# A fused attention and feed-forward kernel: two groups of transposes moved from TensorE to DMA, the loads of the next batch moved forward, half chunks widened to 128 rows

## The chip, the cores and the metric

The kernel runs on one core of one Trainium2 chip. The metric is the device time of one execution in microseconds (us). A time is the median of several executions; a profile is one execution, and its span is about 2 us shorter than the device time. "Before" is the tuned kernel, "the changed kernel" has the change.

## The reference

```python
# attention: batch 8, heads 8, sequence 576, head dimension 64
theta = pi/2 * pos / S
phi(x) = concat(relu(x) * cos(theta), relu(x) * sin(theta))     # 128 features
kv  = einsum('bhsf,bhsd->bhfd', phi(k), v);  z = sum_s phi(k)
num = einsum('bhsf,bhfd->bhsd', phi(q), kv); den = einsum('bhsf,bhf->bhs', phi(q), z)
x   = (num / den) as (4608 tokens, 512)
# feed-forward
out = ((x @ w1) * (x @ w2)) @ w3 @ w_out        # 512 -> 1024 -> 1024 -> 512
```

The inputs are float32, the kernel computes in bfloat16 and gives float32.

## The kernel before

A batch is worked in five chunks of its sequence: four of 128 rows and one of 64, the half chunk, whose number is 4. The features of q and x have to be transposed, so that the features and not the rows of the sequence lie across the partitions. TensorE (PE) does it as a matmul against the identity, followed by a copy out of PSUM, or a DMA does it. The feed-forward part (FFN) works in nine tiles of 512 tokens; the attention of later batches is threaded between its matmuls at fixed slots.

```python
def order_of(b):
    return [0, 1, 2, 3, 4] if b % 2 == 0 else [4, 0, 1, 2, 3]

def dma_q(b):                        # chunks of q that a DMA transposes
    return order_of(b)[5 if b == 0 else 2 if b == 1 else 0:]

def num(b, c):                       # shortened
    nt = ps_att.tile([P, 2, 512], FP32, name="pnum")      # one buffer
    for h in range(H):
        nc.tensor.matmul(nt[...], lhsT=qpT[:, h, ds(at, 128)], rhs=kvs[:, h, :], ...)
    # VectorE: den = nt[.., 64] + 1e-6; reciprocal; xblk[rows] = nt[rows] * den

def x_tr(b, c):                      # shortened
    if b >= 2:
        nc.sync.dma_start_transpose(out=xT[t][:, :, ds(o, R)], in_=xf)
        return
    for kc in range(4):
        nc.tensor.transpose(pst[:, kc, 0:R], xf[:, ts(kc, 128)], identb[rows, rows])
    copy(out=xT[t][:, :, ds(o, R)], in_=pst[:, 0:4, 0:R])
...
# the last tile: its stores go out by SyncE and ScalarE in turn
if t == NT - 1:
    store((nc.sync, nc.scalar)[ms % 2], osb[:, ms % 2:ms % 2 + 1, :], 4 * t + ms, 1)
```

## Time and profile before

| | before |
|---|---|
| device time, median | 249.42 us in 3 runs; 249.39 with a fourth, beside the changed kernel |
| span of the profile | 247.4 us |
| PE busy | 239.9 us, 97% |
| VectorE / ScalarE / GpSimd busy | 57% / 50% / 38% |
| PE in the chain that ended last | 92% |
| matmuls of 512 columns | start 216 ns apart |
| transposes of 128 columns | start 56 ns apart |

The chain follows back from the last instruction to whatever released each step. Where it consists of PE pieces that touch, PE is the bound. (Ends of matmuls are modelled and overlap, so in a timeline I reckon with 216 ns per matmul of 512 columns and not with the length shown.) In the notation of the profile "PE ffnps L464 x8" is eight matmuls of line 464 that write the tile ffnps, SPq is an issue by SyncE, and the bracket at the end of a line of a timeline is how long the engine stood idle before it and what ended that.

### The profile page before, as it was taken

How to read it: one execution, taken by the hardware profiler on the slowest of the kernel's cores; microseconds unless marked ns; L12 is line 12 of the kernel's file. 1: busy time of each engine (PE TensorE's matmuls, PEld its weight loads, DVE VectorE, ACT ScalarE, POOL GpSimd, SP SyncE). 2: the span in 40 equal slices, each digit the busy share in tenths (PEclk: the TensorE clock that was granted, in tenths of full speed). 3: DMA queues.
4: the chain of work that ended last, by engine and by line, in shares of the span. 5: the costliest groups of instructions: out<-in, count | busy, mean ns of one | idle time of the engine just before them, and what ended most of it. 6: DMA issues, size and time to landing. Idle time of an engine off the chain costs nothing.

```text
span 247.4 us, 4896 instructions
## 1 busy us (share of the span) xinstructions
PE 239.9 (97%) x1808; PEld 127.5 (52%) x1839; DVE 141.9 (57%) x333; ACT 123.2 (50%) x209; POOL 94.3 (38%) x189
## 2 busy tenths in 40 slices
PE   8899999999999999999999999999999999999994
PEld 2478555565554445544544455455545554444443
DVE  7776674656657555748465966566586555312421
ACT  2676325927852594267426832783287332323331
POOL 7755241215512442154113621562143008878100
PEclk9999999999999999999999999999999999999999
DMA  6999999999999999999989899999985938999413
GB/s 195 179 193 199 210 204 205 144 160 190 181 119 194 138 154 133 149 158 174 124 134 151 112 153 153 153 181 146 141 108 150 185 82 170 305 300 303 154 41 130
DMA packets 86087, 41.15 MB, mean 166 GB/s; under 512 B 53552, under 2 KB 82608, under 8 KB 86064
## 3 DMA queue, kind: packets, MB, share of 16 engines
q0 software_dynamic: 37072, 27.20, 72.7%
q1 hardware_dynamic: 48560, 13.18, 33.4%
q10 hardware_dynamic: 432, 0.46, 0.5%
q8 instruction: 14, 0.23, 0.4%
q14 instruction: 9, 0.07, 0.1%
HBM read 38.80 MB, written 9.44 MB: 195 GB/s over the span
## 4 chain that ended last, share of the span: by engine, by line
PE 92%; DMA 3%; issue 1%; DVE 1%; POOL 1%; ACT 0%; POOLq 0%
PE ffnps L464 50%; PE ffnps L510 24%; PE ffnps L232 5%; PE pnum L355 4%; PE pnum L297 4%; DMA qs<-in_q_dram 3%; PE pst L220 2%; PE pst L392 1%; PE pst L328 1%; PE ffnps L527 1%; POOL vs L112 0%; DVE xblk L365 0%; PE pfirst L355 0%; ACT xT L394 0%; DVE xT L394 0%
## 5 line engine op out<-in xcount | busy, mean ns | idle before, releaser
L505 DVE TENSOR_TENSOR abT<-asb,ffnps 128x512 bf16<-128x512 bf16 x68 | 46.6, 685 | 56.1 <-PE ffnps L464 55.9
L464 PE MATMUL ffnps<-xT,w1b 128*128 128x512 bf16 (+2 forms) x310 | 74.4, 357 | 0.9 <-ACT xT L394 0.2
L464 PE MATMUL ffnps<-xT,w2b 128*128 128x512 bf16 (+2 forms) x312 | 74.0, 357 | 0.4
L510 PE MATMUL ffnps<-w34b,abT 128*128 128x512 bf16 x271 | 64.7, 379 | 0.4
L501 ACT CAST asb<-ffnps 128x512 bf16<-128x512 f32 x68 | 39.8, 585 | 49.8 <-PE ffnps L464 48.4
L516 ACT COPY held<-ffnps 128x512 f32<-128x512 f32 x35 | 20.5, 586 | 49.6 <-PE ffnps L510 43.6
L464 PEld LDWEIGHTS <-w1b 128*128 128x128 bf16 x320 | 28.9, 98 | 27.7 <-issue 0.6
L464 PEld LDWEIGHTS <-w2b 128*128 128x128 bf16 x320 | 28.7, 98 | 26.9
L510 PEld LDWEIGHTS <-abT 128*128 128x128 bf16 x280 | 25.6, 98 | 26.4
L269 ACT ACTIVATE qp<-qs,sinv 128x512 bf16<-128x512 bf16 (+2 forms) x40 | 28.3, 715 | 2.1 <-DMA qs<-in_q_dram 2.0
L365 DVE TENSOR_TENSOR xblk<-pnum,den 128x512 bf16<-128x512 f32 (+1 forms) x39 | 26.9, 691 | 2.2
L269 ACT ACTIVATE kp<-ks,sinv 128x512 bf16<-128x512 bf16 (+1 forms) x35 | 24.5, 720 | 0.0
L438 POOL DMA_DIRECT2D out_dram<-held x42 | 22.1, 532 | 4.6 <-DMA out_dram<-held 1.8
L540 POOL COPY seen<-xblk 64x1 bf16<-64x1 bf16 x15 | 2.7, 183 | 53.4 <-DVE xblk L365 53.4
L355 PEld LDWEIGHTS <-qpT 128*128 128x128 bf16 x320 | 15.0, 98 | 10.2 <-issue 2.7
L540 POOL COPY seen<-qp 64x1 bf16<-64x1 bf16 x14 | 2.6, 183 | 40.6 <-DVE qp L265 40.6
L265 DVE TENSOR_SCALAR qp<-qs,cosv 128x512 bf16<-128x512 bf16 (+1 forms) x40 | 17.2, 434 | 1.2 <-DMA qs<-in_q_dram 1.2
L363 DVE TENSOR_SCALAR den<-pnum 128x8 f32<-128x8 f32 (+1 forms) x39 | 6.4, 164 | 19.4 <-PE pnum L355 19.4
L289 POOL COPY va<-vs 128x512 bf16<-128x512 bf16 (+1 forms) x30 | 17.5, 632 | 0.0
L297 PEld LDWEIGHTS <-kp 128*128 128x128 bf16 x280 | 13.0, 98 | 7.3
L355 PE MATMUL pnum<-kvs,qpT 128*128 128x65 bf16 x312 | 16.4, 194 | 0.2
L232 PE MATMUL ffnps<-woutb,w3T 128*128 128x512 bf16 x61 | 15.0, 379 | 0.1
(87 smaller groups left out, 184.2 us busy)
## 6 DMA issues: line engine op xcount, KB each, us to landing
out_dram<-held POOLq DMA_DIRECT2D x16, 256.0 KB, 4.6
out_dram<-held POOLq DMA_DIRECT2D x24, 128.0 KB, 3.9
qs<-in_q_dram POOLq DMA_DIRECT2D x10, 256.0 KB, 5.6
w3b<-in_moe_w_dram POOLq DMA_DIRECT2D x8, 256.0 KB, 13.4
ks<-in_k_dram POOLq DMA_DIRECT2D x8, 256.0 KB, 6.0
vs<-in_v_dram POOLq DMA_DIRECT2D x8, 256.0 KB, 6.4
ks<-in_k_dram POOLq DMA_DIRECT2D x6, 320.0 KB, 5.5
qs<-in_q_dram POOLq DMA_DIRECT2D x6, 320.0 KB, 5.3
```

What stands on the lines that cost most here:

```text
L232: nc.tensor.matmul(acc[:, :], lhsT=w3T[:, lc, :], rhs=woutb[:, lc, :], start=(lc == 0), stop=(lc == 7))
L269: nc.scalar.activation(out=dst[:R, c, 0:n, D:F], in_=src[:R, 0:n, c, :], func=ACTF.Relu, scale=sinv[:R, at:at + 1], bias=0.0)
L289: eng.tensor_copy(out=feat_of(b)[2][:R, c, :, 0:D], in_=raw[b, "v"][:R, :, c, :])
L297: nc.tensor.matmul(kvt[:, h // 4, ds((h % 4) * 65, 65)], lhsT=kp[:, c, h, :], rhs=va[:, c, h, 0:D + 1], start=(i == 0 and h % 4 == 0), sto ...
L355: nc.tensor.matmul(nt[:, h // 4, ds((h % 4) * 65, 65)], lhsT=qpT[:, h, ds(at, 128)], rhs=kvs[:, h, :], start=True, stop=True)
L365: nc.vector.tensor_tensor(out=xblk[rows], in0=n4[:, :, :, 0:D], in1=den[rows].unsqueeze(3).to_broadcast([R, 2, 4, D]), op=ALU.mult)
L438: eng.dma_start(out=rows[:, :, cols], in_=osb[64 * i:64 * i + rows.shape[0], :, cols])
L464: nc.tensor.matmul(out, lhsT=w[:, kc, ts(jc, 128)], rhs=x[:, kc, tok], start=(kc == 0), stop=(kc == 3))
L501: nc.scalar.copy(out=asb[:], in_=aT[:, :])
L505: nc.vector.tensor_mul(out=abT[:, jc, :], in0=asb[:], in1=bT[:, :])
L510: nc.tensor.matmul(ops[:, :], lhsT=abT[:, jc, ts(ms, 128)], rhs=w34b[:, jc, :], start=(jc == 0), stop=(jc == 7))
L516: nc.scalar.copy(out=osb[:, ms % 2, :], in_=ops[:, :])
```

## The change

The intent is to shorten PE's stream: batch 1 takes its half chunk second instead of first, so that four of its five query chunks can go by DMA (a); x of its chunk 3 goes by DMA too (b); the x transposes of the two half chunks on PE use 128 rows instead of 64 (c); keys, values and queries of batch 2 are loaded sooner (d).

```diff
@@ other_loads
         load(1, "qv")
+        load(2, "k", 0)
@@ order_of, dma_q
+        if b == 1:
+            return [0, 4, 1, 2, 3]
-        return order_of(b)[5 if b == 0 else 2 if b == 1 else 0:]
+        return order_of(b)[5 if b == 0 else 1 if b == 1 else 0:]
@@ num
+        if b < 2 and c == 4:
+            rows, R = slice(0, P), P
+            n4 = nt[rows, :, 0:260].rearrange("p g (h e) -> p g h e", e=65)
@@ x_tr
+        xa = xblk[:].rearrange("p g h d -> p (g h d)")
-        if b >= 2:
+        if b >= 2 or b == 1 and c == 3:
-            nc.tensor.transpose(pst[:, kc, 0:R], xf[:, ts(kc, 128)], identb[rows, rows])
+            nc.tensor.transpose(pst[:, kc, :], xa[:, ts(kc, 128)], identb[:])
-        copy(out=xT[t][:, :, ds(o, R)], in_=pst[:, 0:4, 0:R])
+        copy(out=xT[t][:, :, ds(o, R)], in_=pst[:, 0:4, rows])
@@ slots of batch 1
-                         nu=(15, 17, 19, 20, 25), xt=(20, 20, 21, 22, 27))
+                         nu=(15, 17, 19, 20, 25), xt=(20, 20, 21, 22, 25))
-            for i in range(2):
-                between[11 + i].append(lambda i=i: behind_q(1, 2 + 2 * i, 2, "k", i))
-            for i, g in enumerate((15, 17, 17, 19)):
-                between[g].append(lambda i=i: behind_x(1, (i + 1) // 2, 2, "vvqq"[i], i % 2))
+            between[10].append(lambda: behind_q(1, 0, 2, "k", 1))
+            between[14].append(lambda: behind(att[1]["kvs"][0:64, 0, 0:1], 2, "v", 0))
+            for i, g in enumerate((15, 17, 17)):
+                between[g].append(lambda i=i: behind_x(1, (i + 1) // 2, 2, "vqq"[i], (1, 0, 1)[i]))
```

## The prediction

> **What bounds the kernel now.** I read the page's busy shares first, then the chain that ended last, then the chain and the timelines around 28 to 31 us and 44 to 82 us, where the change acts.
>
> ```profile
> PE 239.9 (97%) x1808; PEld 127.5 (52%) x1839; DVE 141.9 (57%) x333; ACT 123.2 (50%) x209; POOL 94.3 (38%) x189
> PE 92%; DMA 3%; issue 1%; DVE 1%; POOL 1%; ACT 0%; POOLq 0%
> ```
>
> The first line is busy time by engine, the second the shares of the chain. TensorE (PE) is both the busiest engine and 92% of the chain; VectorE, ScalarE and GpSimd are each under 60%. Busy time alone would not prove it, since matmuls overlap in the pipeline, so I looked at the rhythm in the chain (start, length, what):
>
> ```profile
> 46.71 0.45 PE pst L220 x8
> 48.02 0.45 PE pst L328 x8
> 48.47 0.86 PE ffnps L232 x4
> 49.33 0.45 PE pst L328 x8
> 49.78 0.86 PE ffnps L232 x4
> 50.64 1.27 PE pnum L297 x40
> ```
>
> Each piece starts where the one before ends: four matmuls of 512 columns take 0.86 us (216 ns each), eight transposes of 128 columns 0.45 us (56 ns each). There is no wait here. So PE streams columns without a pause, and a column removed from its stream is time off the end, provided that no operand comes late. The trace's start times say the same over the whole run: apart from lost records, from 31 us to the end I find pauses over 60 ns at only a dozen places, together about 1.5 us. The kernel has no 2% (5.0 us) to give in the part that the change touches.
>
> **What the Trainium skill says.** "TensorE: Matmul & The Clock Gate", section "Step-by-step: what each phase is for", gives 215.7 ns between matmuls of 512 columns and 55.6 ns for 128; the trace agrees (216 and 56). (The section after it says 131 and 81 for real kernels; this trace does not show that.) Its section "Part 4: PE-mode transpose" gives some 275 ns for a 128x128 transpose in a kernel. That is the duration of one; the trace has 219 ns for it, and in a stream they start 56 ns apart, so 56 ns is what I charge. "TensorEngine Tiling (Array Packing)", "Key Properties", says that changing the tiling mode drains TensorE. The trace agrees: the 64-row transposes of a half chunk are surrounded by two gaps (below). "DMA: Bandwidth & Descriptors", "Issuing engines are not separate DMA queues", says that all queues end on the same 16 DMA engines and interleave; the trace agrees, as a DMA transpose of q issued among loads landed after 6.3 us (median), among fewer after 3.0.
>
> **The change part by part.** I set the order of each engine's instructions against that of before. On PE 12 of 1839 matmuls (and their weight loads) go and 8 get wider. On the DMA queue of SP two transposes come in. VectorE loses one copy, ScalarE one copy, GpSimd one tiny copy.
>
> *(a) The half chunk of q of batch 1 by DMA.* Eight transposes of 128 columns go at about 49.3 us: 8 x 56 ns = 0.45 us, all of it PE stream, as the lines above show. VectorE loses a 0.42 us copy. The copy of the 128-row chunk (0.68 us) now stands ahead of the v copies, which ended at 50.24; by VectorE's line they would start about 49.25 (when the second half of v lands, 49.24) and the first be done at 49.6, the last about 50.45. PE reaches the kv matmuls about 50.1 and eats one chunk in 0.26 us, so it wants the last at 51.1. No wait.
>
> *(b) x of chunk 3 of batch 1 by DMA.* Four transposes go:
>
> ```profile
> 64.54 1.03 PE L464 MATMUL ffnps<-xT,w2b 128*128 128x512 bf16 x4
> 64.73 0.69 DVE L365 TENSOR_TENSOR xblk<-pnum,den 128x512 bf16<-128x512 f32 x1
> 65.47 0.23 PEld L392 LDWEIGHTS <-xblk 128*128 128x128 bf16 x4 [0.40 <-DVE xblk L365]
> 65.47 0.40 PE L392 MATMUL pst<-identb,xblk 128*128 128x128 bf16 x4
> ```
>
> In this timeline the matmuls from 64.54 are streamed by 64.54 + 4 x 0.216 = 65.40, but the transposes start at 65.47, just after xblk is written (65.42): a wait of 0.07 us. With it go 4 x 56 = 0.22 us. Saved: 0.29 us. This x belongs to the third 512-token tile of the FFN, read far later (about 109 us), so the DMA has 40 us.
>
> *(c) Half chunks with 128 rows.* Two places, batch 0 at 30.24 us and batch 1 at 57.88:
>
> ```profile
> 29.28 1.03 PE L464 MATMUL ffnps<-xT,w1b 128*128 128x512 bf16 x4
> 30.24 0.29 PE L392 MATMUL pst<-identb,xblk 64*128 64x64 bf16 x4
> 30.46 1.04 PE L464 MATMUL ffnps<-xT,w2b 128*128 128x512 bf16 x4
> ```
>
> The stream before ends at 29.28 + 0.86 = 30.14; the next begins at 30.46. The half chunk costs 0.32 us, though its 4 x 64 columns are only 0.12: two gaps of about 95 ns as the array changes its rows. With 128 rows the columns double to 4 x 56 = 0.22 and the gaps go: 0.09 us saved. In batch 1 the same 0.09 is saved in the stream but not in time: the next matmuls of PE write the one pnum buffer, and wait for VectorE to have normalized the chunk before. That xblk write ends at 58.26 and they start at 58.40, after a pause of 0.06 already; the pause just grows. So (c) is worth 0.09, not 0.18. VectorE's operations on 128 partitions instead of 64 cost the same (0.69 and 0.68 us).
>
> *(d) Loads of batch 2 sooner.* These move no PE work and PE waits for no load after 20 us in this trace, so alone they are worth nothing. They matter as room for (a), and because PE will want everything 0.8 us sooner:
>
> ```profile
> 38.23 0.68 POOL L137 DMA_DIRECT2D vs<-in_v_dram  x1 [0.97 <-DMA ks<-in_k_dram]
> 47.07 0.18 POOL L540 COPY seen<-qp 64x1 bf16<-64x1 bf16 x1 [8.16 <-DVE qp L265]
> 47.52 0.68 POOL L133 DMA_DIRECT2D ks<-in_k_dram  x1 [0.27 <-issue]
> ```
>
> GpSimd issues nothing for eight microseconds, waiting for a q feature, and the DMA engines run dry: between 48.0 and 49.5 us they moved 33 GB/s, against 176 just before. The lower half of k now follows v directly and fills that hole, the upper half follows at about 47.5 instead of 48.9, and v and q come about 2 us sooner, one step of the attention each.
>
> Sum: 0.45 + 0.29 + 0.09 = 0.83 us, 249.42 - 0.83 = 248.59.
>
> **The rivals.** *First: the DMA transposes of q come late.* There are now four in a row, the half chunk first, with deadlines of about 54.2 (half), 56.2 (chunk 1) and 57.9 (chunk 2), which are the starts of before less 0.45. Before, chunks 1, 2 and 3 were issued at 48.2, 49.6 and 52.3 and landed at 54.5, 57.6 and 58.5, so chunk 2 landed only 0.8 us before its use at 58.40. ScalarE now has its feature of chunk 1 about 0.6 us later, since the half chunk's 0.72 us activation no longer runs before the upper half of q lands, and SP issues the half chunk before it. Against it: the three landings were slow because both halves of k came in between (52.2 and 57.0); k will be through by about 52. But v of batch 2 now comes in from 53 to 58. If chunk 2 is late, it costs 0.3 to 1.2 us and most of the gain is gone: 248.9 to 249.6. I give it one in four. *Second: the pauses of batch 2 change.* PE stood 0.16, 0.07 and 0.16 us at 76.0, 78.1 and 80.2, each time until VectorE had normalized the chunk before; the order there is unchanged, and the same pauses recur in later batches, so I expect them to stay. Should a shift by 0.8 us remove them, 248.2. *Third: the gain is taken back downstream,* by a load or store that does not move with PE: against it, later loads are all triggered by the compute, and the chain has no DMA in it after 12 us. It would give 249.3 or so. *Fourth: VectorE or ScalarE bounds this stretch,* for (c) it does; for (a) and (b) the PE lines show no such wait.
>
> **Range and chances.** From 248.59 I move up 0.06 for the first rival: 248.65. The low end is the full gain, both halves of (c) and some of the pauses gone; the high end is a late transpose that takes nearly all. The runs of before lie within 0.4 us, which adds to both ends: 248.1 to 249.4. A gain or loss of 2% needs 5 us, and nothing here is of that size, so within 2% is nearly certain.
>
> **What would show it.** Twelve fewer matmuls and weight loads on PE; kv matmuls of batch 1 starting about 0.5 us sooner, near 50.1 in the chain; no 64-row transposes; a pause before the fourth num group of batch 1 grown from 0.06 to about 0.15; everything from 70 us on about 0.8 us sooner; the hole in DMA at 48 us filled. I am wrong if PE pauses at the num groups of the half chunk or of chunks 1 and 2 of batch 1 on the landing of a q transpose, if the v copies hold the kv matmuls, or if PE's later pauses grow by what was saved.

## The result, and the profile after

The changed kernel took 249.0 us (248.8 to 249.21, four runs), the kernel before 249.39 us (249.21 to 249.6, four runs). The ratio is 0.9984, with a 95% interval from 0.9967 to 1.0001. A ratio is the mean time of one kernel's runs over that of the other's of the same rounds, so it is not quite the ratio of the medians. Some 0.4 us were gained where 0.8 was expected. In two later groups of runs the unaltered changed kernel came out at 1.0004 and 0.9998 of the kernel before, so even the 0.4 us are not certain.

First, what the page of the changed kernel says (busy time, then the shares of the chain):

```profile
PE 241.2 (98%) x1827; PEld 127.2 (51%) x1827; DVE 142.1 (57%) x332; ACT 122.5 (50%) x208; POOL 93.9 (38%) x188
PE 92%; DMA 3%; DVE 1%; issue 1%; POOL 1%; ACT 0%; POOLq 0%
```

PE looks busier although it does less: the trace of before has 1808 of 1839 matmuls, here all 1827 are recorded. A comparison of busy sums would mislead by more than the effect, so I compare start times. The chain of the changed kernel, around the transposes that went (start, length, what):

```profile
46.92 0.45 PE pst L221 x8
47.37 0.86 PE ffnps L233 x4
48.23 0.45 PE pst L331 x8
48.68 1.73 PE ffnps L233 x8
50.40 1.27 PE pnum L300 x40
```

One group of eight transposes is left where there were two, and eight matmuls now run in one piece. From the start of those transposes to the kv group it is 2.17 us (48.23 to 50.40); before it was 2.62 us (48.02 to 50.64). That is 0.45 us for (a), and the v copies cause no wait. The timeline around the half chunk of batch 0, and the one around the last x of batch 1:

```profile
29.59 1.03 PE L472 MATMUL ffnps<-xT,w1b 128*128 128x512 bf16 x4
30.46 0.39 PE L400 MATMUL pst<-identb,xblk 128*128 128x128 bf16 x4
30.68 1.03 PE L472 MATMUL ffnps<-xT,w2b 128*128 128x512 bf16 x4
```

```profile
64.30 1.03 PE L472 MATMUL ffnps<-xT,w2b 128*128 128x512 bf16 x4
64.48 0.69 DVE L372 TENSOR_TENSOR xblk<-pnum,den 128x512 bf16<-128x512 f32 x1
65.16 0.81 PE L472 MATMUL ffnps<-xT,w1b 128*128 128x512 bf16 x3
65.20 1.19 SPq L395 DMA_TRANSPOSE xT<-xblk  x1
```

In the first, four transposes take 0.22 us and both neighbours touch them: 29.59 + 0.86 = 30.45. The two gaps are gone. In the second, PE goes straight from one group of matmuls to the next (64.30 + 0.86 = 65.16) while SyncE issues the transpose. And GpSimd's loads:

```profile
38.48 0.68 POOL L137 DMA_DIRECT2D vs<-in_v_dram  x1 [0.57 <-DMA ks<-in_k_dram]
39.85 0.68 POOL L133 DMA_DIRECT2D ks<-in_k_dram  x1 [0.69 <-DMA ks<-in_k_dram]
46.85 0.18 POOL L548 COPY seen<-qp 64x1 bf16<-64x1 bf16 x1 [6.32 <-DVE qp L268]
47.30 0.68 POOL L137 DMA_DIRECT2D ks<-in_k_dram  x1 [0.27 <-issue]
```

The lower half of k follows v at 39.85 instead of 47.52, and between 48.0 and 49.5 us the DMA engines moved 170 GB/s instead of 33.

So every expected step is there. To see where the gain ended, I cut the span at five places that can be found in every trace: the first FFN matmul, the first kv group of batch 2, the last matmul, the landing of the last store, the end (us; the table also has the experiments told below).

```
                     first FFN   to kv of   to last   to last   to the    span
                     matmul at   batch 2    matmul    landing   end
before                 15.85      51.59     176.63     2.34      0.99    247.40
changed                16.16      50.74     176.62     2.32      1.36    247.19
after_again            15.92      50.74     177.27     2.33      1.34    247.59
after_third            15.51      50.74     179.32     2.33      1.35    249.24
after_tiny7            15.91      50.73     177.45     2.36      0.92    247.37
after_pool_store       15.82      50.73     176.84     2.35      0.93    246.67
after_pool_store2      15.82      50.74     176.99     2.38      0.93    246.86
after_late_x           15.76      50.73     176.79     2.36      0.92    246.55
after_no_b27           16.08      51.04     176.63     2.31      0.92    246.98
after_no_b             15.74      52.77     176.62     2.32      0.93    248.37
after_no_d             16.03      54.68     177.60     2.32      1.35    251.97
before_tiny2           15.92      51.59     176.63     2.38      1.34    247.86
part_c                 15.79      51.49     177.27     2.34      0.98    247.86
part_b                 15.61      51.28     176.99     2.33      0.92    247.13
```

Second column: the change took 51.59 - 50.74 = 0.85 us off PE's stream, against 0.83 predicted, and it did so in every execution, within 0.01 us. Last column but one: 0.37 us of it are lost after the last store has landed. The start of this one execution was 0.31 us later. The third column is the same here, but not in the repeats.

The 0.37 us after the landing can be followed in the semaphore instructions of SyncE at the end. In these traces the hardware DMAs (those issued by SyncE and ScalarE) take eight completion semaphores in turn. At the end SyncE waits for all of them in a fixed order, one after another, about 62 ns each where nothing is outstanding. Times at which these waits ended:

```
semaphore     1st     2nd     3rd     4th     5th     6th     7th     8th    last landing
before      244.67  244.73  244.79  245.74  246.11  246.28  246.45  246.52   246.41 (7th)
changed     245.88  245.94  246.00  246.07  246.13  246.19  246.25  246.31   245.83 (1st)
```

The change adds two hardware DMAs, so the last store moves two places on, from the seventh semaphore past the eighth to the first. Before, SyncE had done six of the eight waits when the last store landed; now all eight are still to do. The summary of SyncE's waits shows the same in one line each, before and changed (us in total, times, longest):

```profile
SPq L690 <- DMA out_dram<-held: 1.2, 2, 0.9
```

```profile
SPq L698 <- DMA out_dram<-held: 1.8, 1, 1.8
```

Before, the two waits counted are those on the fourth and the fifth semaphore (0.90 and 0.32 us in the trace); those for the last two stores, 0.13 us each, are too short for this view. In the changed kernel it waits once, 1.8 us, on the first of the eight, and by then all others are done.

### The profile page after: what moved, and what is told of

Same layout as the page of the kernel before. It is cut to its first block, busy times and chain, and to the rows that moved or that the text cites. A ratio compares the mean times of both kernels' runs of the same rounds, so it can differ in the third digit from the quotient of the medians.

```text
span 247.2 us, 4909 instructions
## 1 busy us (share of the span) xinstructions
PE 241.2 (98%) x1827; PEld 127.2 (51%) x1827; DVE 142.1 (57%) x332; ACT 122.5 (50%) x208; POOL 93.9 (38%) x188
## 4 chain that ended last, share of the span: by engine, by line
PE 92%; DMA 3%; DVE 1%; issue 1%; POOL 1%; ACT 0%; POOLq 0%
PE ffnps L472 50%; PE ffnps L518 24%; PE ffnps L233 6%; PE pnum L358 4%; PE pnum L300 4%; DMA qs<-in_q_dram 3%; PE pst L221 1%; PE pst L400 1%; PE ffnps L535 1%; PE pst L331 1%; POOL vs L112 0%; DVE xblk L372 0%; PE pfirst L358 0%; ACT xT L402 0%; DVE xT L402 0%
## 5 line engine op out<-in xcount | busy, mean ns | idle before, releaser
L472 PE MATMUL ffnps<-xT,w2b 128*128 128x512 bf16 (+2 forms) x320 | 74.9, 357 | 0.0
L518 PE MATMUL ffnps<-w34b,abT 128*128 128x512 bf16 x280 | 65.8, 379 | 0.0
```

Of the source, the lines that this page charges most:

```text
L472: nc.tensor.matmul(out, lhsT=w[:, kc, ts(jc, 128)], rhs=x[:, kc, tok], start=(kc == 0), stop=(kc == 3))
L518: nc.tensor.matmul(ops[:, :], lhsT=abT[:, jc, ts(ms, 128)], rhs=w34b[:, jc, :], start=(jc == 0), stop=(jc == 7))
```

## The experiments

My theory after the result (the closing theory): PE's stream gained 0.85 us as predicted, and 0.37 to 0.43 us went to the order of the closing waits. The rivals: the start got slower by 0.31 us through the change; or the difference is noise; or, as the prediction feared, late DMA transposes take the gain back in the middle.

### First group: the closing waits

**after_again** is the changed kernel once more.

> The changed kernel, unaltered, as the yardstick of this group. Both theories: ratio to before 0.998 (0.997 to 1.000). Closing theory: from the landing of the last store to the end of the span 1.36 us again, with eight more semaphore waits of SyncE after that landing. Start theory (the changed kernel lost 0.3 us because its first load of k landed at 7.32 instead of 6.76 us): if the change did that, it lands near 7.3 again and PE's first FFN matmul starts near 16.15; if it is scatter from run to run, it moves.

Measured: 249.34 us (249.07 to 250.7, 6 runs), before 249.37 (248.86 to 251.31, 11 runs), ratio 1.0004 (0.9977 to 1.0030). Landing to end 1.34 us. The first load of k landed at 6.85 us and PE's first FFN matmul was at 15.92. In a third profile of the same kernel, told below, they were 6.45 and 15.51. The start is scatter: the rival of the start falls. But this execution lost 0.65 us in the third column. By the start times PE stood 0.25 us before the third FFN tile (at 85.4 us) and 0.38 us before the fourth (at 109.0), each time until a DMA transpose of x had landed; more on this in the third group.

**after_tiny7** adds seven useless DMAs, to turn the semaphores on by seven.

```diff
     load_first4(nc.sync, k0, k)
+    junk = const.tile([16, 7, 16], FP32, name="junk")
+    for i in range(7):
+        nc.sync.dma_start(out=junk[:, i, :], in_=q[0, 0, ds(16 * i, 16), 0:16])
```

> The changed kernel with seven DMAs of 1 KB each, whose data nobody reads, issued by SyncE behind the first loads, so that the last store of the output takes the eighth of the eight completion semaphores of the hardware queues instead of the first. Closing theory: SyncE has one wait left after the last landing instead of eight, landing to end 0.93 us instead of 1.36, and the time about 0.4 us under the changed kernel's, 248.6, ratio to before 0.9966. Rival (the missing gain went to the start or to noise): the time of the changed kernel, 249.0, ratio 0.998 to 0.999.

Measured: 249.26 us (248.47 to 249.7), ratio 0.9988 (0.9963 to 1.0012). Landing to end 0.92 us, with one wait left, as the theory has it. The time of 248.6 did not come: in the profiled execution 0.83 us were lost in the third column. The closing part of the expectation held, the time did not show it.

**after_pool_store** reaches the same without extra DMAs.

```diff
-                store((nc.sync, nc.scalar)[ms % 2], osb[...], 4 * t + ms, 1)
+                store((nc.gpsimd, nc.scalar, nc.sync)[ms], osb[...], 4 * t + ms, 1)
```

> The changed kernel with the first store of the last 512-token tile issued by GpSimd instead of SyncE. There is one hardware DMA fewer, so the last store again takes the eighth semaphore, without any extra DMA. Closing theory: landing to end 0.93 us, time about 248.6, ratio 0.9966, and the same as with the seven small DMAs. Rival: 249.0, or slower if GpSimd's store lands last.

Measured: 248.83 us (248.59 to 249.72), ratio 0.9981 (0.9956 to 1.0007). Landing to end 0.93 us; GpSimd's store landed at 242.0 us, well before the others. The median is 0.51 us under that of after_again, in the right place, but the intervals overlap.

**before_tiny2** gives the kernel before the two extra hardware DMAs and nothing else (the same edit as in after_tiny7 with 2 in place of 7).

> The kernel before with two DMAs of 1 KB, whose data nobody reads, issued by SyncE behind the first loads: as many more hardware DMAs as the change adds, and nothing else of it. Closing theory: the last store takes the first semaphore, landing to end goes from 0.99 to 1.36 us, time 249.75, ratio 1.0015, while PE's stream is as before. Rival: no change, ratio 1.0000.

Measured: 249.68 us (249.3 to 250.45), ratio 1.0011 (0.9988 to 1.0034). Landing to end 1.34 us instead of 0.99, the stream 51.59 us as before. So two DMAs that move 2 KB lengthen the closing by 0.35 us in the profile. In all fourteen traces the closing follows from the last store's semaphore alone: 0.92 to 0.93 us on the eighth, 0.98 to 0.99 on the seventh, 1.34 to 1.36 on the first. That part is shown, for profiled executions; the device times agree in direction but are too wide to show it by themselves.

### Second group: the parts

**part_c**, the kernel before with the widened half chunks alone (the edits of num and of the PE branch of x_tr above).

> The kernel before with (c) alone: the two half chunks of x with 128 rows. By the prediction's reckoning 0.09 us off PE's stream at 30 us (first FFN matmul to first w3 transpose 16.26 instead of 16.35 us) and nothing at 58 us, where the pause before the fourth num group of batch 1 grows from 0.06 to about 0.16 us. No DMA is added, so landing to end stays 0.99 us. Ratio to before 0.9996, too little for the times to show. Rival (both half chunks pay): 0.18 us in the stream.

Measured: 249.42 us against 249.23 for before on this chip, ratio 1.0004 (0.9985 to 1.0022). The stream is 0.10 us shorter, all of it at 30 us; at 58.2 us the pause is 0.17 us. So one half chunk pays and the other does not, and the rival falls. The profiled execution also had a pause of 0.46 us at 177.6 us on a late DMA transpose of q: such pauses come without the change's DMAs too.

**part_b**, the kernel before with x of chunk 3 of batch 1 by DMA.

```diff
-        if b >= 2:
+        if b >= 2 or b == 1 and c == 3:
```

> The kernel before with (b) alone: x of chunk 3 of batch 1 by DMA. Stream 0.29 to 0.30 us shorter between the last num group of batch 1 and the first kv group of batch 2. One hardware DMA more, so by the closing theory the last store takes the eighth semaphore and landing to end is 0.93 us instead of 0.99. Sum 0.36 us, ratio 0.9986: nearly all of what the whole change gained in the record's times. Rival for a cost of (b): the transpose stands ahead of those of q of batch 2 on SyncE, so chunk 1 of that q, which landed 2.3 us before its use in the kernel before, has 1 us or less left, and in some executions PE waits for it.

Measured: 249.27 us, ratio 1.0002 (0.9977 to 1.0026). The stream is 51.59 - 51.28 = 0.31 us shorter and the closing 0.92 us, both as expected. But the time does not show the 0.36 us. The profile has the cost that the rival named: chunk 1 of q of batch 2 landed at 75.03 instead of 73.74 us, 0.46 us before its use, and at 80.03 PE waited 0.34 us more than usual for another chunk:

```profile
PE pnum L355 <- DMA qpT<-qp: 0.3, 1, 0.3
```

**after_no_b**, the changed kernel with the line of part_b undone.

> The changed kernel without (b): x of chunk 3 of batch 1 on PE again. PE's stream is 0.30 us longer than the changed kernel's, and one hardware DMA goes, so by the closing theory landing to end falls from 1.36 to 0.93 us: the time comes out about 0.13 us under the changed kernel's though PE does more work; stream 0.55 us shorter than before, ratio to before 0.9975. Rival (closing order does not matter): 0.3 us slower than the changed kernel. The landing of chunk 1 of q of batch 2 should again be 1.5 us or more ahead of its use.

Measured: 250.14 us (249.92 to 250.85), ratio 1.0039 (1.0012 to 1.0065). Slower than the kernel before, and than the changed kernel in each of its groups, against the expectation. The list of PE's waits names the cause:

```profile
PE pst L400 <- DVE xblk L372: 1.6, 1, 1.6
```

The experiment was wrong. The change had also moved this x from slot 27 to slot 25, right behind its own num group. A DMA doesn't mind, but PE then stands and waits until VectorE has normalized the chunk. Closing: 0.93 us, as expected. A part has to be undone together with the place that was chosen for it.

**after_no_d**, the changed kernel with the loads of batch 2 where the kernel before has them (the first part of the diff and the loads in its last part undone).

> The changed kernel without (d): k, v and q of batch 2 loaded when the kernel before loaded them. If (d) is the room that (a) needs: chunk 2 of q of batch 1 lands after 58 us and PE pauses 0.3 to 1 us at its num group, the DMA engines move about 33 GB/s between 48.0 and 49.5 us as before, ratio to before 0.999 to 1.002. If (d) is worth nothing: stream as in the changed kernel, landing to end 1.36 us, ratio 0.998.

Measured: 251.59 us (250.53 to 253.86), ratio 1.0102 (1.0043 to 1.0162). The first theory holds, and the cost is larger than I expected: by the medians, of different groups, (d) is worth some 2.5 us to the changed kernel. The profiled execution is the longest of the four (253.86 us); its stream to batch 2 is 3.94 us longer than the changed kernel's. The busy time by stretch (PE, its weight loads, VectorE, ScalarE, GpSimd, then the granted clock, the DMA share and GB/s), and one line of PE's timeline:

```profile
56.20:58.70 2.50, 0.26 (x2) 0.00 (x0) 0.00 (x0) 0.80 (x2) 1.65 (x4) 1.00 1.57 102
58.70:60.60 1.90, 1.84 (x20) 1.37 (x21) 1.30 (x4) 0.65 (x2) 0.11 (x1) 0.84 1.38 212
60.60:63.60 3.00, 2.78 (x20) 1.74 (x19) 1.35 (x5) 1.91 (x5) 1.62 (x4) 0.53 1.57 134
```

```profile
58.76 0.43 PE L357 MATMUL pnum<-kvs,qpT 128*128 128x65 bf16 x8 [2.30 <-DMA qpT<-qp]
```

It was chunk 1, not chunk 2, that came late: its transpose, issued at 49.37 us, landed at 58.72 us, while both halves of k came in. PE stood 2.3 us, and then its granted clock fell: 0.53 on average from 60.60 to 63.60 us, where matmuls of 512 columns started up to 427 ns apart. The expectation didn't contain that. From 48.0 to 49.5 us the DMA engines moved 32 GB/s: the hole is back.

```profile
48.00:49.50 1.50, 1.50 (x15) 0.91 (x14) 1.27 (x3) 1.50 (x3) 1.30 (x3) 1.00 0.20 32
```

### Third group: what (b) costs, and two versions that beat the kernel before

**after_third** is the changed kernel again.

> The changed kernel, unaltered, as the yardstick of this group. Landing to end 1.36 us, eight waits of SyncE after the last landing; stream from the first FFN matmul to the first kv group of batch 2 50.73 us (51.59 before). Ratio to before 0.998 to 1.000.

Measured: 249.09 us (248.57 to 251.3), before 249.14 (249.05 to 250.98, 11 runs), ratio 0.9998 (0.9963 to 1.0034). The stream to batch 2 and the closing are as expected. The profiled execution was the longest one, of 251.3 us, and shows why (PE's waits, and its timeline):

```profile
PE ffnps L472 <- DMA xT<-xblk: 2.3, 2, 1.6
```

```profile
82.62 2.32 PE L518 MATMUL ffnps<-w34b,abT 128*128 128x512 bf16 x10
86.56 1.02 PE L472 MATMUL ffnps<-xT,w1b 128*128 128x512 bf16 x4 [1.61 <-DMA xT<-xblk]
```

The third FFN tile could not start, because two x transposes of batch 2 landed at 86.2 and 86.4 us, 8.8 and 7.5 us after their issue. In the first profile of the same kernel PE started that tile at 85.38, and the last of these transposes had landed at 85.18:

```profile
82.78 2.75 PE L518 MATMUL ffnps<-w34b,abT 128*128 128x512 bf16 x12
85.38 1.03 PE L472 MATMUL ffnps<-xT,w1b 128*128 128x512 bf16 x4
```

**after_no_b27** undoes (b) with its slot.

```diff
-        if b >= 2 or b == 1 and c == 3:
+        if b >= 2:
-                         nu=(15, 17, 19, 20, 25), xt=(20, 20, 21, 22, 25))
+                         nu=(15, 17, 19, 20, 25), xt=(20, 20, 21, 22, 27))
```

> The changed kernel without (b), this time with the place of the transposes restored too: the change had also moved x of chunk 3 next to its own num group, which is harmless for a DMA but makes PE wait 1.8 us for VectorE (that spoiled the first trial). Now the transposes stand two steps later, as in the kernel before. Closing theory: stream 0.55 us shorter than before, landing to end 0.93 us, ratio 0.9975 to 0.9985, at least as fast as the changed kernel although PE does 0.3 us more. Rival: 0.3 us slower than the changed kernel.

Measured: 248.60 us (248.56 to 248.93, 6 runs), ratio 0.9968 (0.9945 to 0.9990). The stream is 51.59 - 51.04 = 0.55 us shorter than before and the closing 0.92 us. PE does 0.30 us more than in the changed kernel, and the kernel is faster than before by an interval that leaves out 1, which none of the three groups of the changed kernel did. The gain is 0.3%, far under 2%. Its six runs lie within 0.4 us, those of the changed kernel beside it within 2.7; but those of before, also without (b), lie within 1.9, so the spread alone does not point at (b). No wait on a DMA stands in its list of PE's waits.

**after_pool_store2** is after_pool_store once more.

> The changed kernel with the first store of the last tile issued by GpSimd, once more, beside the changed kernel on one chip. Closing theory: landing to end 0.93 us, 0.43 us under the changed kernel, ratio to before 0.9966 to 0.998. Rival: no better than the changed kernel.

Measured: 248.98 us (248.32 to 249.35), ratio 0.9976 (0.9948 to 1.0004). Closing 0.93 us. The median is only 0.11 us under after_third's; the mean is 0.57 us lower, but much of that is the one run of 251.3 us. This version has the same closing as after_no_b27, and so is the fairer one to hold it against: without (b) the median is 0.38 us lower and the mean 0.20, though PE does 0.30 us more. The runs of the two overlap, so this is a hint and not a proof that (b) costs more than it saves.

**after_late_x** is after_pool_store with x of chunk 3 issued behind the q transposes of batch 2.

```diff
+            if b == 2 and i == 0:
+                plan[z + 7].append(lambda: x_tr(1, 3))        # and no longer at slot 25
             plan[z + 7 + 2 * i].append(lambda c=c: x_tr(b, c))
```

> The same, and the DMA transpose of x of chunk 3 of batch 1 issued behind those of q of batch 2 instead of ahead of them. If its place in the queue is what made chunk 1 of q of batch 2 late (landing 0.2 to 0.3 us before its use, once 0.2 us after it): that chunk lands about 1.3 us before its use, and PE does not wait for it. Risk: the three x transposes of batch 2 that the third FFN tile reads at 85.4 us go out later, and PE may wait there 0.1 to 0.5 us. Landing to end 0.93 us. Ratio 0.996 to 0.998 if the risk stays out.

Measured: 248.67 us (248.42 to 249.1), ratio 0.9968 (0.9945 to 0.9992), with after_no_b27 the best. But the reason I gave for it missed: chunk 1 of q landed at 75.19 us, 0.05 us before its use at 75.24, and PE's pause there was 0.31 us instead of 0.16. The place in SyncE's queue alone does not explain the landing.

Laying the traces side by side, I found what goes with it: how long before GpSimd's load of v for batch 3 the transpose of chunk 1 was issued.

```
                                           issued ahead of v     issue to landing
after_no_b27, part_c, after_no_b,
before_tiny2                                0.88 to 1.24 us        3.2 to 3.4 us
before                                      0.70                   5.1
after_late_x                                0.45                   7.3
changed, after_again, after_third, after_tiny7,
after_pool_store, after_pool_store2, part_b  -0.49 to -0.04        5.8 to 6.6
```

All kernels with (b) in its place issue chunk 1 after v. The issue times show two parts of it. SyncE is busy 1.2 us with x; counted from the first FFN matmul, chunk 1 is issued 0.6 to 1.0 us later in the six traces of the changed kernel with (b) in its place than in after_no_b27. And (b) lets PE, and with it the trigger of the v load, run 0.3 us sooner. This is a pattern over thirteen executions; I did not isolate it by moving v alone.

## Why the prediction was right or wrong

The time lay in the range and within 2%, as predicted. That says little: the range of 248.1 to 249.4 takes in the kernel before as well (249.39), and the direction was right but not clear of the noise, and the repeats show no gain. The central value of 248.65 us was too low by 0.35 us against the run on record, by more against the repeats.

*"So PE streams columns without a pause, and a column removed from its stream is time off the end, provided that no operand comes late."* The first half held to 0.02 us: 0.85 us measured between the first FFN matmul and batch 2, against 0.83. By parts: (a) 0.45, as worked out; (b) 0.30 to 0.31 against 0.29; (c) 0.10 against 0.09, and nothing in batch 1, where the pause before the num group grew from 0.06 to 0.17 us just as reckoned. The second half failed. "Time off the end" does not follow when the end itself depends on the count of DMAs: the closing grew by 0.37 us. The prediction counted the two added transposes on the queue and gave them no cost at the end. The proviso did not hold either, in most executions with (b), as told below under the first rival. (A slip beside it: from 31 us on I now count ten pauses over 60 ns in the trace of before, 1.1 us in all, not a dozen and 1.5 us.)

*"This x ... read far later (about 109 us), so the DMA has 40 us."* This was wrong. The third tile is read at 85.4 us; the fourth is the one at about 109. The x itself still had 16 us to spare (landing 69.3 us) and never held PE. If it cost anything, it was by what stood behind it: the transposes of batches 2 and 3, a case that I had not listed.

*First rival, transposes of q late.* I looked for it in batch 1, where it did not come: in the changed kernel the half chunk and chunks 1, 2 and 3 landed 1.5, 2.6, 1.8 and 2.2 us before their use. It came in batch 2. Of the eight traced executions with (b), leaving out after_no_d, seven lost 0.17 to 2.7 us in the third column; of the five without (b) one did (part_c, 0.65 us). By the start times nearly all of it is PE's waiting for late transposes: of q at num groups of batch 2 (part_b, after_pool_store, after_late_x), and of x before the third FFN tile (after_again, after_third) or the fourth (these two, after_tiny7, after_pool_store2); after_tiny7 waited for q of a later batch too. That (b) makes such pauses more frequent is therefore likely, but not shown. The last x transpose for the fourth tile took 4.9 to 6.0 us in the six traces of the changed kernel with (b) in its place, and 4.1 us in after_no_b27; but it took only 3.8 us in part_b, which has (b) alone. How much (b) costs on average is not settled: an execution is one draw, and why some x transposes took 8.8 us is open.

*"(d) ... alone they are worth nothing. They matter as room for (a)."* The second sentence was right and mattered more than I wrote: without (d) the median is some 2.5 us higher. In the profiled execution, the longest of the four, the stream is 3.94 us longer: one wait of 2.3 us, and the stretch at a lower clock behind it.

*Second and fourth rival.* The pauses of batch 2 at the num groups stayed, at 0.16, 0.07 and 0.16 us, as expected. VectorE bounds only the place named in (c).

*Third rival, the gain taken back downstream.* It was put at a low weight because the chain has no DMA in it. The chain starts from the last instruction that does work and so leaves out the landing of the last store and the waits after it, which is exactly where 0.37 us went.

## What to carry to other kernels

When a gain is smaller than a microsecond, cut the span at fixed places and compare the pieces, since the whole time mixes the start, the stream, late DMAs and the closing. Check what an added DMA does to the order in which completions are waited for at the end, and to the transfers that queue behind it; a transpose moved off the busiest engine may cost more there than it saved. And when one part of a change is undone for a test, undo the place in the schedule that was chosen for it as well.

## What the Trainium skill lacked or had wrong

- No page has the cost of the closing waits: SyncE waited for the completion semaphores one after another, 62 ns each, and from the landing of the last store to the end passed 0.92 to 0.93 us with that store on the last of eight hardware semaphores, 1.34 to 1.36 us with it on the first.
- "TensorEngine Tiling (Array Packing)", section "Key Properties", says that a change of the tiling mode drains TensorE, but gives no cost: the 64-row transposes of a half chunk had gaps of 93 to 96 ns on either side.
- "TensorE: Matmul & The Clock Gate", section "Back-to-back issue gap", gives 131 and 81 ns between matmuls of 512 and 128 columns in real kernels; this kernel had 216 and 56 ns at the full clock, which is what the same page calls the isolated case.
- The same page, section "Why this matters for your kernels", warns of pauses over some 3 us; here, in one execution, a pause of 2.3 us was enough: the granted clock then averaged 0.53 over 3 us (after_no_d). After pauses of 1.6 us (after_no_b, after_third) the matmuls went on 216 ns apart.
